# Sliding-window half of a decode attention kernel, regrouped from four units of four heads to two units of eight

## The chip, the cores and the metric

The kernel runs on one core of a Trainium2 chip. A core has a matrix engine (PE, with its weight loads listed as PEld), a vector engine (VectorE, DVE in the profile), a scalar engine (ScalarE, ACT), GpSimd (POOL) and a synchronisation engine (SyncE, SP), which here issues nearly all transfers. The engines have instruction streams of their own and wait for one another on semaphores. Sixteen DMA engines move data from device memory to the on-chip memory of 128 partitions; matmul results go to eight accumulation banks of 128 x 512 floats. The metric is the device time of one execution in microseconds (us), lower is better.

## What is computed

Two independent attention layers for one new token, A and B, of the same sizes: 576 inputs, 32 query heads, 16 key-value heads of 128 channels, a cache of 8192 keys in bf16. A looks only at the last 2048 keys, B at all.

```python
B, Sq, D = 1, 1, 576
Hq, Hkv, Sk, Dh = 32, 16, 8192, 128
W = min(4096, max(256, Sk // 4))        # A only: 2048
q = (x @ wq) as 32 heads of 128
k = jnp.repeat(k_cache[:, :, Sk - W:, :], 2, axis=1)   # B: all of k_cache
v = jnp.repeat(v_cache[:, :, Sk - W:, :], 2, axis=1)
scores = jnp.einsum("bhqd,bhkd->bhqk", q, k) * (Dh ** -0.5)
p = softmax(scores)
o = jnp.einsum("bhqk,bhkd->bhqd", p, v)
return o.reshape(B, Sq, Hq * Dh) @ wo   # A and B side by side: 1152 numbers
```

The bytes that must be read are A's and B's wq and wo, 8.4 MB each of K and V for A (16 heads x 2048 keys x 128 channels x 2 bytes), and 33.6 MB each of K and V for B.

## The kernel before

**Order of work.** The class `Prog` (L39) collects operations by engine; each engine runs its list in the order in which the program appended it, and `emit` (L61) turns named dependencies into semaphore waits. So the order of the calls at L466 to L492 is the order on every engine.

**Loads.** `place` (L172) hands out space in `ring`, 73728 bf16 columns on 128 partitions, from left to right, going back to 0 when a piece would not fit. A load waits for the last users of the space that it overwrites. All of these loads are issued by SyncE in one order: wo of A (its first part, in a buffer of its own), the two parts of wq for A and B, then K and V of the units as L234 to L237 give it (K of unit i, then V of unit i-1), then the rest of wo. Since one queue takes them all, a load that waits on SyncE holds up the ones behind it.

**Units.** A unit is a group of key-value heads, four of A or four of B (L213); units 0 to 3 are A's and 4 to 7 are B's. A partition of an A unit holds head p % 4 and 64 keys in one row of 16 KB (L222), in a single load of 2 MB for K and for V. A B unit has rows of 64 KB, K in two loads of 4 MB and V in one of 8 MB, the last unit's V in two. A load is named by kind and unit, with its half: K5.1 is the second half of K of unit 5.

**Slabs.** A unit's row is worked in slabs of 2048 columns, that is 16 keys a partition: four slabs for an A unit, sixteen for a B unit. For each slab VectorE transposes K (`turn`, L360) in 32 x 32 blocks into one of three slots of `ktb`; PE then multiplies it (`score`, L367) by four shifted views of the query in `za` or `zb`, so that each slab's scores fall on rows of their own in one bank of 128 x 512 floats. For A a first matmul (L373) with `mkl` and `mkr` puts a large negative number wherever query head and key head do not belong together.

**Softmax of a unit.** `peak` (L394): the maximum over the bank (max) on VectorE and a transposing matmul (mT) on PE. `spread` (L401): VectorE takes the maximum by query head (mr) and scales it (mx), PE spreads it to all partitions (bc). `expo` (L414): ScalarE copies it (nb) and takes the exponential into `psb`, with a running sum. `turnp` (L424): VectorE transposes p into `pta` (A) or `pts` (B). `pv` (L436): four matmuls a slab, each with 32 columns of p and 512 columns of V, into four groups of 32 rows of one bank. `take` (L450) copies the bank to `xo` on ScalarE, and `fold` (L455) adds the groups up on PE.

**How units overlap.** While a unit goes through its softmax, K of the next one is transposed and scored: in the loop at L469, one slab after `peak`, one after `spread`, one after `expo`, and the rest after `turnp`. Only then, in PE's order, come the PV matmuls of the unit, so a V buffer comes free after the scores of the next unit.

**Ends.** Before the units, q is made by matmuls as wq lands (L315 to L331), copied by ScalarE, transposed by VectorE (L332) and put into `za` (L338) and `zb` (L343); the first K transpose waits for both. After them the sums are inverted (L496 to L513) and the output is multiplied by wo (`final`, L518), part by part as wo lands.

Of the kernel before, what the change touches and what calls it, by code (L numbers as in the profile page):

```python
# [11 lines left out]
HQ = 32  # L12
# [11 lines left out]
TA = 4 * W_A // 128  # L24
# [3 lines left out]
ZA = 128 + 24  # L28
# [71 lines left out]
def bass_concat_heads__sliding_block_cached__gqa_block_cached__decode_kernel(nc, A_x, A_k_cache, A_v_cache, A_wq, A_wo,  # L100
# [21 lines left out]
    za = nc.alloc_sbuf_tensor("za", [128, NQ, 4, ZA], BF16)  # L122

    mkl = nc.alloc_sbuf_tensor("mkl", [4, 16, 4, 2], BF16)
    mkr = nc.alloc_sbuf_tensor("mkr", [4, 128, 4], BF16)
    mx = nc.alloc_sbuf_tensor("mx", [128, 8], F32)
    mr = nc.alloc_sbuf_tensor("mr", [128, 8], F32)

    pta = nc.alloc_sbuf_tensor("pta", [128, NA, 16, 8], BF16)
    rsa = nc.alloc_sbuf_tensor("rsa", [128, NQ], F32)  # L130
    clsa = nc.alloc_sbuf_tensor("clsa", [128, 8], F32)
    mexp = nc.alloc_sbuf_tensor("mexp", [1, 128], F32)
    nb = nc.alloc_sbuf_tensor("nb", [128, 4], F32)
    psb = nc.alloc_sbuf_tensor("psb", [128, 512], BF16)
# [4 lines left out]
    sel = nc.alloc_sbuf_tensor("sel", [128, 32], F32)  # L139
    par = nc.alloc_sbuf_tensor("par", [128, 2], F32)  # L140
# [72 lines left out]
    UNITS = [(side, u) for side in "AB" for u in range(NQ)]  # L213
# [3 lines left out]
    def load_kv(kind, i):  # L217
        side, u = UNITS[i]
        c = (ks if kind == "K" else vs)["AB".index(side)]
        use = "T%d.%d" if kind == "K" else "V%d.%d"  # L220
        if side == "A":
            src = bass.AP(tensor=c.tensor, offset=c.offset + (4 * u * SK + SK - W_A) * DH,  # L222
                          ap=[[TA * DH, 32], [SK * DH, 4], [1, TA * DH]])
            kv_at[kind, i] = [place(TA * DH, [use % (i, NA - 1)], lambda e, t: e.dma_start(t, src), "%s%d.0" % (kind, i))]
            return
        rows = c[0, 4 * u:4 * u + 4, :, :].rearrange("h (q t) d -> (h q) (t d)", q=32)
        n = 2 if kind == "K" or i == NU - 1 else 1
        kv_at[kind, i] = []
        for half in range(n):
            src = rows[:, half * ROW // n:(half + 1) * ROW // n]  # L230
            kv_at[kind, i].append(place(ROW // n, [use % (i, (half + 1) * NB // n - 1)],
                                        lambda e, t, src=src: e.dma_start(t, src), "%s%d.%d" % (kind, i, half)))
# [41 lines left out]
    op("pool", lambda e: e.tensor_copy(mkr[:], view(ident, 128, 0, [[0, 128], [1, 4]], 4)), deps=["ident"], name="mkr")  # L274
# [16 lines left out]
    for k0 in range(0, KW, 4):  # L291
# [10 lines left out]
    op("dve", lambda e: e.tensor_reduce(clsa[:], view(identf, 128, 0, [[1, 8], [8, 16]]), AX.X, ALU.add),  # L302
       deps=["identf"], name="clsa")
    op("dve", lambda e: e.tensor_reduce(sel[:], view(identf, 128, 0, [[1, 32], [32, 4]]), AX.X, ALU.add),
       deps=["identf"], name="sel")
    op("dve", lambda e: e.tensor_scalar(mkl[:], view(ident, 128, 0, [[0, 16], [1, 4], [0, 2]], 4), -1.0, BIG,
# [14 lines left out]
    for n in range(8):  # L321
# [5 lines left out]
        for h in range(2):  # L327
            op("act", lambda e, n=n, h=h: e.activation(qsb[:, n, 256 * h:256 * h + 256],  # L328
                                                       banks[n][:, 256 * h:256 * h + 256], ACT.Copy),
               deps=["qmm%d" % (KW0 + n)], name="qe%d" % n if h else None)  # L330
# [6 lines left out]
    for b in range(4):  # L337
        op("dve", lambda e, b=b: e.tensor_copy(  # L338
            view(za, NQ * 4 * ZA, ZA - 128 + 32 * b, [[4 * ZA, NQ], [2 * ZA, 2], [ZA, 2], [1, 8]], 32, 32 * b),
            view(ktb, KT, 0, [[1024, NQ], [64, 2], [1, 2], [128, 8]], 32, 32 * (b % 2))),  # L340
            deps=QT + ["za0"], name="z0.%d" % b)
    for b in range(4):
        op("dve", lambda e, b=b: e.tensor_copy(  # L343
            view(zb, NQ * 4 * ZW, 32 * b + W0, [[4 * ZW, NQ], [2 * ZW, 2], [ZW, 2], [1, 2]], 32, 32 * b),
            view(ktb, KT, b * 256, [[1024, NQ], [64, 2], [1, 2], [128, 2]], 32, 64 + 32 * (b % 2))),
            deps=QT + ["zb0"], name="z1.%d" % b)
# [5 lines left out]
    sbank = [(qb if side == "A" else sb)[u % 2] for side, u in UNITS]  # L352
    vbank = [vb[1] if side == "A" else vb[0] for side, _ in UNITS]

    def prev(i):

        return [i - 2] if i >= 2 and UNITS[i - 2][0] == UNITS[i][0] else []
# [9 lines left out]
    def score(i, s):  # L367
        side, u = UNITS[i]
        k, bank = k0[i] + s, sbank[i]

        def mm(e):
            if side == "A" and s == 0:
                e.matmul(bank[:, :], lhsT=mkl[:].rearrange("p a h r -> p (a h r)"),  # L373
                         rhs=mkr[:].rearrange("p q h -> p (q h)"), start=True, stop=False)
            for c in range(2):
                for v in range(2):
                    if side == "A":
                        lhsT = za[:, u, 2 * c + v, ZA - 128 - 8 * s:ZA - 8 * s]
                    else:
                        lhsT = zb[:, u, 2 * c + v, W0 - 2 * s:W0 - 2 * s + 128]  # L380
# [3 lines left out]
                                   stop=(s == nslab[i] - 1 and c == 1 and v == 1))  # L384
            return ins
        deps = ["T%d.%d" % (i, s)]
        if s == 0:
            deps += ["mkl", "mkr"] + QE
            for n in prev(i):
                deps += ["exp%d" % n, "max%d" % n]  # L390
        op("pe", mm, deps=deps, name="S%d" % k)


    def peak(i):  # L394
        was = ["mr%d" % (i - 1), "nb%d" % (i - 1)] if i else ["identf"]
        op("dve", lambda e: e.tensor_reduce(mx[:, 0:1], sbank[i][:, :], AX.X, ALU.max),  # L396
           deps=["S%d" % (k0[i] + nslab[i] - 1)] + (["mT%d" % (i - 1)] if i else []), name="max%d" % i)
        op("pe", lambda e: e.matmul(mb[0:1, 0:128], lhsT=mx[:, 0:1], rhs=identf[:, :], start=True, stop=True),  # L398
           deps=["max%d" % i] + was, name="mT%d" % i)

    def spread(i):  # L401
        A = UNITS[i][0] == "A"
        deps = ["mT%d" % i] + (["mx%d" % (i - 1), "bc%d" % (i - 1)] if i else [])
        rows = [[1, 8], [8, 16]] if A else [[32, 4], [1, 2], [2, 16]]
        out = mr[0:1, :] if A else mr[0:1, :].rearrange("p (b r) -> p b r", r=2)
        op("dve", lambda e: e.tensor_reduce(out, view(mb, 512, 0, rows, parts=1), AX.X, ALU.max), deps=deps,  # L406
           name="mr%d" % i)
        to, of = ([[8, 16], [1, 8]], [[0, 16], [1, 8]]) if A else ([[32, 4], [2, 16], [1, 2]], [[2, 4], [0, 16], [1, 2]])
        op("dve", lambda e: e.tensor_scalar(view(mexp, 128, 0, to, parts=1), view(mr, 8, 0, of, parts=1), -SCALE, None,
# [4 lines left out]
    def expo(i):  # L414
# [3 lines left out]
           deps=["bc%d" % i] + (["exp%d" % (i - 2)] if i >= 2 else []), name="nb%d" % i)  # L418
        acc = (rsa if side == "A" else rsb)[:, u:u + 1]
        op("act", lambda e: e.activation(psb[:, :], sbank[i][:, :], ACT.Exp, bias=nb[:, c:c + 1], scale=SCALE,  # L420
                                         accum_out=acc),
           deps=["nb%d" % i, "warm1"] + (["PT%d" % (i - 1)] if i else []), name="exp%d" % i)

    def turnp(i):  # L424
        side, _ = UNITS[i]
        deps = ["exp%d" % i, "pts0"] + (["V%d.%d" % (i - 1, nslab[i - 1] - 1)] if i else [])
        if side == "A":
            op("dve", lambda e: e.transpose(view(pta, NA * 128, 0, [[8, 16], [128, NA], [1, 8]]), psb[:, :]),  # L428
               deps=deps, name="PT%d" % i)
        else:  # L430
            for b in range(4):
                op("dve", lambda e, b=b: e.transpose(  # L432
                    view(pts, NB * 128, 2 * b, [[8, 16], [128, NB], [1, 2]], 32, 32 * b), psb[32 * b:32 * b + 32, :]),
                   deps=deps, name="PT%d" % i if b == 3 else None)

    def pv(i, s):  # L436
        src, landed = slab("V", i, s)

        def mm(e):
            for j in range(4):  # L440
                if UNITS[i][0] == "A":
                    lhsT = pta[:, s, 4 * j:4 * j + 4, :].rearrange("p t k -> p (t k)")
                else:
                    lhsT = view(pts, NB * 128, 128 * s + 32 * j, [[1, 32]])
                ins = e.matmul(vbank[i][32 * j:32 * j + 32, :], lhsT=lhsT, rhs=src[:, 512 * j:512 * j + 512],  # L445
                               start=(s == 0), stop=(s == nslab[i] - 1))
            return ins
        op("pe", mm, deps=[landed, "PT%d" % i] + (["xo%d" % (i - 1)] if i else []), name="V%d.%d" % (i, s))
# [6 lines left out]
    def fold(i):  # L455
        side, u = UNITS[i]
        c, at = (1, 8 * u) if side == "A" else (0, HQ + 8 * u)

        def mm(e):
            for t in range(4):  # L460
                ins = e.matmul(ob[:, at:at + 8], lhsT=xo[:, c, 128 * t:128 * t + 128], rhs=sel[:, 8 * t:8 * t + 8],  # L461
                               start=(t == 0), stop=(t == 3))
            return ins
        op("pe", mm, deps=["xo%d" % i, "sel"], name="O%d" % i)

    for s in range(nslab[0]):  # L466
        turn(0, s)
        score(0, s)
    for i in range(NU):  # L469
# [3 lines left out]
        def ahead(m):  # L473
            for s in todo[:m]:
                turn(i + 1, s)
                score(i + 1, s)
# [10 lines left out]
        turnp(i)  # L487
# [7 lines left out]
    last = NU - 1  # L495
    op("dve", lambda e: e.tensor_tensor(  # L496
        lsel[:, 0, :].rearrange("p (u m) -> p u m", m=8), rsa[:, :].unsqueeze(2).to_broadcast([128, NQ, 8]),
        view(clsa, 8, 0, [[0, NQ], [1, 8]]), ALU.mult), deps=["exp%d" % (NQ - 1), "clsa"], name="lselA")
    op("dve", lambda e: e.tensor_tensor(
        lsel[:, 1, :].rearrange("p (u m) -> p u m", m=8), rsb[:, :].unsqueeze(2).to_broadcast([128, NQ, 8]),  # L500
        view(clsb, 8, 0, [[0, NQ], [1, 8]]), ALU.mult), deps=["exp%d" % last, "clsb"], name="lsel")
# [16 lines left out]
    def final(P, c):  # L518
# [10 lines left out]
        op("pe", mm, deps=["wo%d.%d" % (P, c), "oP", "exp%d" % (NQ - 2)], name="F%d.%d" % (P, c))  # L529
# [44 lines left out]
```

## Time and profile before

| | |
|---|---|
| median of three runs | 246.12 us (246.03 to 246.19) |
| the profiled execution | 245.95 us |
| its span, first to last instruction | 244.6 us |
| mean granted PE clock | 0.847 |
| busy: PE, VectorE, ScalarE, GpSimd | 69%, 51%, 9%, 3% |
| read from device memory | 102.76 MB, 420 GB/s over the span |
| transposes of K on VectorE (L364) | 80, 92.8 us in all |
| transposes of p for A (L428), each | 712 ns |
| maximum over an A bank (L396), each | 692 ns |
| loads of A's K and V | eight, 2048 KB each |

A page of the profile shows one execution. Its digits give the busy share in tenths in 40 slices of the span. A queue's line gives packets, megabytes and the share that its packets took of sixteen engines over the span. In the chain of waits each step is followed back to what released it; a step of a transfer lasts from its issue to its landing, so it can span other transfers that went ahead of it in the queue. A line of the timeline has the start, the duration, and in brackets the idle time of the engine before it and what ended it.

### The profile page before, as it was taken

How to read it: one execution, taken by the hardware profiler on the slowest of the kernel's cores; microseconds unless marked ns; L12 is line 12 of the kernel's file. 1: busy time of each engine (PE TensorE's matmuls, PEld its weight loads, DVE VectorE, ACT ScalarE, POOL GpSimd, SP SyncE). 2: the span in 40 equal slices, each digit the busy share in tenths (PEclk: the TensorE clock that was granted, in tenths of full speed). 3: DMA queues.
4: the chain of work that ended last, by engine and by line, in shares of the span. 5: the costliest groups of instructions: out<-in, count | busy, mean ns of one | idle time of the engine just before them, and what ended most of it. 6: DMA issues, size and time to landing. Idle time of an engine off the chain costs nothing.

```text
span 244.6 us, 2224 instructions
## 1 busy us (share of the span) xinstructions
PE 168.2 (69%) x952; PEld 69.5 (28%) x952; DVE 124.7 (51%) x156; ACT 21.5 (9%) x54; POOL 8.1 (3%) x15
## 2 busy tenths in 40 slices
PE   0059692977887799669736569938197976654696
PEld 0024240322444222323112323203052322321453
DVE  0040026677688998899700679930369960130200
ACT  2200052001121100200000010000010000200000
POOL 8400000000000000000000000000000000000000
PEclk9999899579999999979968767997855995757769
DMA  7999899999999999998989999989999999999994
GB/s 279 429 486 435 367 431 429 429 429 437 434 439 434 425 437 445 429 490 386 482 375 429 429 485 396 461 370 429 426 482 418 439 423 402 431 430 426 422 412 190
DMA packets 4369, 102.90 MB, mean 421 GB/s; under 512 B 516, under 2 KB 648, under 8 KB 904
## 3 DMA queue, kind: packets, MB, share of 16 engines
q1 hardware_dynamic: 4356, 102.76, 98.1%
q8 instruction: 7, 0.11, 0.2%
q14 instruction: 2, 0.02, 0.0%
q10 hardware_dynamic: 4, 0.00, 0.0%
HBM read 102.76 MB, written 0.00 MB: 420 GB/s over the span
## 4 chain that ended last, share of the span: by engine, by line
DMA 61%; PE 21%; DVE 12%; ACT 2%; issue 2%; SPq 2%; DVEq 0%
DMA ring<-in_B_v_cache_dram 39%; DMA ring<-in_B_wo_dram 12%; DMA ring<-in_B_wq_dram 10%; DVE ktb L364 9%; PE vb L445 7%; PE qb L381 5%; PE sb L312 2%; ACT psb L420 1%; DVE pta L428 1%; PE ob L461 1%; PE vb L312 1%; PE qb L312 1%; PE sb L381 1%; SPq L201 1%; PE qb L373 1%
## 5 line engine op out<-in xcount | busy, mean ns | idle before, releaser
L364 DVE STREAM_TRANSPOSE ktb<-ring 128x1024 int32<-128x1024 int32 x80 | 92.8, 1211 | 28.2 <-DMA ring<-in_B_k_cache_dram 27.1
L381 PE MATMUL sb<-ktb,zb 128*128 128x512 bf16 x256 | 73.2, 425 | 23.2 <-DVE ktb L364 20.5
L381 PEld LDWEIGHTS sb<-ktb,zb 128*128 128x128 bf16 x256 | 22.8, 104 | 70.1 <-DVE ktb L364 45.4
L445 PE MATMUL vb<-ring,pts 128*32 128x512 bf16 x256 | 23.6, 546 | 20.6 <-DMA ring<-in_B_v_cache_dram 16.5
L381 PE MATMUL qb<-ktb,za 128*128 128x512 bf16 x64 | 19.3, 448 | 2.8 <-DVE ktb L364 2.8
L445 PEld LDWEIGHTS vb<-ring,pts 128*32 128x32 bf16 x256 | 8.5, 130 | 35.2 <-DMA ring<-in_B_v_cache_dram 18.7
L452 ACT ACTIVATE xo<-vb 128x512 f32<-128x512 f32 x8 | 4.8, 597 | 130.3 <-PE vb L445 130.3
L432 DVE STREAM_TRANSPOSE pts<-psb 32x512 bf16<-32x512 bf16 x16 | 11.3, 704 | 7.7 <-ACT psb L420 7.5
L332 DVE STREAM_TRANSPOSE ktb<-qsb 128x512 int32<-128x512 int32 x4 | 2.8, 711 | 21.8 <-ACT qsb L328 21.8
L461 PEld LDWEIGHTS ob<-sel,xo 128*128 128x128 f32 x64 | 10.0, 226 | 3.4 <-ACT xo L452 2.1
L312 PE MATMUL sb<-ring,xrep 128*128 128x512 bf16 x18 | 7.3, 546 | 5.3 <-DMA ring<-in_B_wq_dram 5.3
L525 PE MATMUL qb<-ring,oP 128*1 128x256 bf16 (+1 forms) x112 | 10.2, 326 | 0.5 <-DMA ring<-in_B_wo_dram 0.5
L461 PE MATMUL ob<-sel,xo 128*128 128x8 f32 x64 | 9.3, 273 | 1.2 <-ACT xo L452 1.2
L381 PEld LDWEIGHTS qb<-ktb,za 128*128 128x128 bf16 x64 | 6.2, 109 | 13.3 <-issue 5.7
L287 PE MATMUL sb<-onesb,xint 1*128 1x128 bf16 x8 | 1.1, 307 | 11.7 <-ACT xint L283 11.7
L525 PEld LDWEIGHTS qb<-ring,oP 128*1 128x1 bf16 x112 | 5.9, 90 | 4.8 <-DMA ring<-in_B_wo_dram 1.7
L539 DVE CAST outsb<-qb 1x256 bf16<-1x256 f32 x2 | 0.8, 420 | 12.1 <-PE qb L525 12.1
L505 DVE RECIPROCAL rl<-mb 128x64 f32<-128x64 f32 x1 | 0.6, 557 | 12.3 <-PE mb L502 12.3
L295 DVE TENSOR_SCALAR xrep<-sb,par 128x256 bf16<-128x256 f32 x4 | 1.7, 477 | 10.1 <-PE sb L287 10.1
L373 PE MATMUL qb<-mkr,mkl 4*128 4x512 bf16 x4 | 1.8, 439 | 7.2 <-DVE ktb L364 7.2
L406 DVE TENSOR_REDUCE mr<-mb 1x8 f32<-1x128 f32 x8 | 1.9, 241 | 9.4 <-PE mb L398 9.4
L396 DVE TENSOR_REDUCE mx<-qb 128x1 f32<-128x512 f32 x4 | 2.8, 692 | 6.3 <-PE qb L381 6.3
(70 smaller groups left out, 86.2 us busy)
## 6 DMA issues: line engine op xcount, KB each, us to landing
ring<-in_B_k_cache_dram SPq DMA_DIRECT2D x8, 4096.0 KB, 24.1
ring<-in_A_k_cache_dram SPq DMA_DIRECT2D x4, 2048.0 KB, 32.6
ring<-in_A_v_cache_dram SPq DMA_DIRECT2D x4, 2048.0 KB, 26.2
ring<-in_B_v_cache_dram SPq DMA_DIRECT2D x2, 4096.0 KB, 23.8
ring<-in_A_wo_dram SPq DMA_DIRECT2D x1, 3456.0 KB, 21.4
ring<-in_A_wq_dram SPq DMA_DIRECT2D x1, 2560.0 KB, 19.4
ring<-in_B_wq_dram SPq DMA_DIRECT2D x1, 2560.0 KB, 24.7
ring<-in_B_wo_dram SPq DMA_DIRECT2D x1, 2448.0 KB, 26.8
```

What stands on the lines that cost most here:

```text
L201: return e.dma_start(bass.AP(tensor=ring, offset=P * RING + lo, ap=[[2 * RING, 64], [1, (k1 - k0) * w]]), src)
L312: return e.matmul(banks[n][:, :], lhsT=xrep[:, k, :], rhs=wq_at[k][:, n * 512:(n + 1) * 512], start=(k == 0), stop=(k == KW - 1))
L332: op("dve", lambda e, n=n: e.transpose(ktb[:, (n - 1) * 512:(n + 1) * 512].bitcast(I32), qsb[:, n - 1:n + 1, :].rearrange("p a n -> p (a n ...
L364: op("dve", lambda e: e.transpose(kt.bitcast(I32), src.bitcast(I32)), deps=[landed] + (["S%d" % (k - NKT)] if k >= NKT else Z), name="T%d. ...
L373: e.matmul(bank[:, :], lhsT=mkl[:].rearrange("p a h r -> p (a h r)"), rhs=mkr[:].rearrange("p q h -> p (q h)"), start=True, stop=False)
L381: ins = e.matmul(bank[:, :], lhsT=lhsT, rhs=view(ktb, KT, (k % NKT) * SLAB + 64 * c + v, [[128, 16], [2, 32]]), start=(side == "B" and s = ...
L396: op("dve", lambda e: e.tensor_reduce(mx[:, 0:1], sbank[i][:, :], AX.X, ALU.max), deps=["S%d" % (k0[i] + nslab[i] - 1)] + (["mT%d" % (i - ...
L432: op("dve", lambda e, b=b: e.transpose(view(pts, NB * 128, 2 * b, [[8, 16], [128, NB], [1, 2]], 32, 32 * b), psb[32 * b:32 * b + 32, :]), ...
L445: ins = e.matmul(vbank[i][32 * j:32 * j + 32, :], lhsT=lhsT, rhs=src[:, 512 * j:512 * j + 512], start=(s == 0), stop=(s == nslab[i] - 1))
L452: op("act", lambda e: e.activation(xo[:, c, :], vbank[i][:, :], ACT.Copy), deps=["V%d.%d" % (i, nslab[i] - 1)] + (["O%d" % (i - 1)] if i e ...
L461: ins = e.matmul(ob[:, at:at + 8], lhsT=xo[:, c, 128 * t:128 * t + 128], rhs=sel[:, 8 * t:8 * t + 8], start=(t == 0), stop=(t == 3))
L525: ins = e.matmul(fb[r:r + 1, 0:hi - lo], lhsT=oP[:, P, k0 + k:k0 + k + 1], rhs=wo_at[P, c][:, k * DM + lo:k * DM + hi], start=(k0 + k == 0 ...
```

## The change

A's sixteen heads are worked in two units of eight heads. Partition 8g + h holds head h of the unit and 128 keys in one row of 32 KB; K and V of a unit are loads of 4 MB. A slab is still 16 keys a partition, so a unit has eight slabs. With sixteen query rows for a slab, two slabs fill a bank, and a unit's scores take four banks, shared in turn with the banks that the projection, B's scores and B's PV use elsewhere in the kernel. Each bank has a mask matmul, a maximum, an exponential and a transpose of its own; a further maximum (top) joins the four. `psb` becomes two of the slots of `qsb`, used in turn. PV of A uses two groups of 64 columns in place of four groups of 32, so a group takes two matmuls of each slab. The copies into `zb` go from four on VectorE to eight on ScalarE, and a reduction (`rta`) adds the four partial sums of each A unit before the inverse is taken. Units 0 and 1 are now A's, 2 to 5 are B's.

```diff
-TA = 4 * W_A // 128
+HA = 8
+UA = G // HA
+TA = HA * W_A // 128
 NA = TA * DH // SLAB
-ZA = 128 + 24
+RA = 2 * HA
+SB = 2
+NBK = NA // SB
+WA = RA * (SB - 1)
+ZA = 128 + WA
...
-    psb = nc.alloc_sbuf_tensor("psb", [128, 512], BF16)
+    psb = qsb
...
-    UNITS = [(side, u) for side in "AB" for u in range(NQ)]
+    UNITS = [(side, u) for side in "AB" for u in range(UA if side == "A" else NQ)]
...
-            src = bass.AP(tensor=c.tensor, offset=c.offset + (4 * u * SK + SK - W_A) * DH,
-                          ap=[[TA * DH, 32], [SK * DH, 4], [1, TA * DH]])
+            src = bass.AP(tensor=c.tensor, offset=c.offset + (HA * u * SK + SK - W_A) * DH,
+                          ap=[[TA * DH, 128 // HA], [SK * DH, HA], [1, TA * DH]])
...
     for b in range(4):
-        op("dve", lambda e, b=b: e.tensor_copy(
-            view(zb, NQ * 4 * ZW, 32 * b + W0, [[4 * ZW, NQ], [2 * ZW, 2], [ZW, 2], [1, 2]], 32, 32 * b),
-            view(ktb, KT, b * 256, [[1024, NQ], [64, 2], [1, 2], [128, 2]], 32, 64 + 32 * (b % 2))),
-            deps=QT + ["zb0"], name="z1.%d" % b)
+        for c in range(2):
+            op("act", lambda e, b=b, c=c: e.activation(
+                view(zb, NQ * 4 * ZW, 32 * b + W0 + 2 * ZW * c, [[4 * ZW, NQ], [ZW, 2], [1, 2]], 32, 32 * b),
+                view(ktb, KT, b * 256 + 64 * c, [[1024, NQ], [1, 2], [128, 2]], 32, 64 + 32 * (b % 2)), ACT.Copy),
+                deps=QT + ["zb0"], name="z1.%d" % b if c else None)
...
-    sbank = [(qb if side == "A" else sb)[u % 2] for side, u in UNITS]
+    for i, (side, u) in enumerate(UNITS):
+        sbank.append([sb[u % 2]] if side == "B" else [(sb[0], vb[0])[u % 2], qb[0], qb[1], sb[1]])
+        before.append([user.get(id(t), []) for t in sbank[i]])
+        nexp.append([sum(map(len, sbank[:i])) + j for j in range(len(sbank[i]))])
+        for j, t in enumerate(sbank[i]):
+            user[id(t)] = ["exp%d.%d" % (i, j), "max%d.%d" % (i, j)]
...
+    def high(i, j):
+        to = mx[:, j:j + 1] if len(sbank[i]) > 1 else mx[:, 4:5]
+        op("dve", lambda e: e.tensor_reduce(to, sbank[i][j][:, :], AX.X, ALU.max),
+           deps=["S%d" % (k0[i] + per(i) * (j + 1) - 1)] + (["mT%d" % (i - 1)] if i else []) +
+           (["top%d" % (i - 1)] if len(sbank[i]) > 1 and i else []), name="max%d.%d" % (i, j))
+
+    def step(i, s):
+        turn(i, s)
+        score(i, s)
+        if s >= 2 * per(i) - 1 and (s + 1) % per(i) == 0:
+            high(i, (s + 1) // per(i) - 2)
...
+        for j, bank in enumerate(sbank[i]):
+            q = nexp[i][j]
+            acc = rsa[:, u, j:j + 1] if side == "A" else rsb[:, u:u + 1]
+            op("act", lambda e, q=q, acc=acc, bank=bank: e.activation(
+                psb[:, q % 2, :], bank[:, :], ACT.Exp, bias=nb[:, c:c + 1], scale=SCALE, accum_out=acc),
+               deps=["nb%d" % i, "warm1"] + (["PT%d.%d" % psof[q - 2]] if q >= 2 else []), name="exp%d.%d" % (i, j))
...
                 if UNITS[i][0] == "A":
-                    lhsT = pta[:, s, 4 * j:4 * j + 4, :].rearrange("p t k -> p (t k)")
+                    lhsT, w, g = pta[:, s, 4 * j:4 * j + 4, :].rearrange("p t k -> p (t k)"), 8 * HA, 2
                 else:
-                    lhsT = view(pts, NB * 128, 128 * s + 32 * j, [[1, 32]])
-                ins = e.matmul(vbank[i][32 * j:32 * j + 32, :], lhsT=lhsT, rhs=src[:, 512 * j:512 * j + 512],
-                               start=(s == 0), stop=(s == nslab[i] - 1))
+                    lhsT, w, g = view(pts, NB * 128, 128 * s + 32 * j, [[1, 32]]), 32, 4
+                ins = e.matmul(vbank[i][w * (j % g):w * (j % g) + w, :], lhsT=lhsT, rhs=src[:, 512 * j:512 * j + 512],
+                               start=(s == 0 and j < g), stop=(s == nslab[i] - 1 and j >= 4 - g))
...
-        turnp(i)
+        for j in range(len(sbank[i])):
+            turnp(i, j)
+            if j % 2 and j < len(sbank[i]) - 1:
+                ahead(1)
...
+    op("dve", lambda e: e.tensor_reduce(rta[:], rsa[:], AX.X, ALU.add), deps=["exp%d.%d" % (UA - 1, NBK - 1)],
+       name="rta")
```

## The prediction

> **What bounds the kernel now.** I read the queues, the digits of the slices and the chain of waits on the page first, then the chain in order of time for its end, then SyncE's issues one by one with the times to landing, and last the timeline from 42 to 98 us, where the change lies.
>
> ```profile
> DMA  7999899999999999998989999989999999999994
> q1 hardware_dynamic: 4356, 102.76, 98.1%
> q8 instruction: 7, 0.11, 0.2%
> DMA 61%; PE 21%; DVE 12%; ACT 2%; issue 2%; SPq 2%; DVEq 0%
> 212.06 29.56 DMA ring<-in_B_wo_dram
> 241.66 1.33 PE qb L525 x12
> 243.01 0.43 ACT outsb L537
> ```
>
> The reader is to see one thing: queue q1 is busy for 98.1% of 16 engines over the span, that is 240.0 of 244.6 us, and the missing 4.6 us lie at the two ends, about 2 us before the first bytes and 3 us after the last. The DMA digits are low only in the first and last slice. The chain ends in the last weights of wo, a matmul, a copy and the store. PE, VectorE and ScalarE stand in that chain only because it hops over them while transfers run behind; their share is not time that can be won. So 102.76 MB through a full queue is the kernel's time, and an edit of the computation counts only if it (a) alters how fast those bytes pass, or (b) delays a load's issue until the queue has run dry.
>
> The margin for (b) is read from SyncE's issues and their landings (columns: start, duration; the other three are one issue each, the last number is us to landing):
>
> ```profile
> 98.02 0.33 SPq L232 DMA_DIRECT2D ring<-in_B_v_cache_dram  x1
> ring<-in_A_v_cache_dram SPq DMA_DIRECT2D x1, 2048.0 KB, 24.7
> ring<-in_B_k_cache_dram SPq DMA_DIRECT2D x1, 4096.0 KB, 20.1
> ring<-in_B_v_cache_dram SPq DMA_DIRECT2D x1, 28.4
> ```
>
> The second is V2, issued at 38.50 and landed at 63.2; the third is K5.1, issued at 86.91 and landed at 107.0; the fourth is V4, issued at 98.02 and landed at 126.4. V4 is the tightest load of the kernel: it is issued 9.0 us before the transfer ahead of it has landed. Every other load after the start has 10 us or more, by the same reckoning (K5.1 itself: issued at 86.91, the load ahead landed at 97.3).
>
> **Bytes and rows.** A's loads go from eight of 2 MB in rows of 16 KB to four of 4 MB in rows of 32 KB; the bytes stay. By the landings, V1, K3 and V2 landed at 53.4, 58.3 and 63.2, so 4.9 us each; B's K halves, 4 MB in 32 KB rows, landed at 97.3 and 107.0, so 9.7 us. Eight times 4.9 is 39.2, four times 9.7 is 38.8: a gain of at most 0.4 us as rounded. The trace's packet records give it finer: by the first of the 16 engines to finish, the eight A loads took 4.86 to 4.89 us each, 39.02 in all, and a B half 9.71, so 38.84 for four: 0.18 us. Their mean packets give the other end: 617 ns for 16 KB and 1218 ns for 32 KB, so 64 x 617 - 32 x 1218 = 0.51 us an engine. I take 0.2, since landings count the overlap of neighbouring packets and single packets do not. On the low side nothing excludes a small loss (below).
>
> **Front end.** z1 (eight ScalarE copies in place of four VectorE copies, 0.79 us in all) now runs beside z0 (1.23 us). An ACT of such a size is bounded by nb's 0.17 us (128x1) and the 0.33 us of a 128x256 copy; at 0.2 it is 8 x 0.23 = 1.85 from 39.92, so the first transpose starts at 41.8 instead of 42.10; at 0.33 it starts at 42.6. Worth nothing either way, as the queue is full until 47 with loads already issued.
>
> **A's computation, walked for when slots come free.** With the ring of 73728 columns the new order places K0 at 36864, K1 at 53248, V0 at 0 (over wq), K2.0 and K2.1 at 16384 and 32768, V1 at 49152, K3.0 at 0, K3.1 at 16384, V2 at 32768 (unit 2 is now B's first). So K2.1 waits for the transposes of K0, V1 for those of K1, K3.0 for PV of unit 0, K3.1 for the first eight transposes of K2, and V2 for the rest of them and for PV of unit 1. From there the places and waits are as before. The bytes ahead of V2 equal those ahead of V4 before, so the queue runs dry at the same moments: 65.8 for K2.1, 75.5 for V1, 85.2 for K3.0, 94.9 for K3.1, 104.8 for V2 (first engine done; the last one 106.6), from the packet records of before with the loads put in the new order.
>
> Rows for the walk:
>
> ```profile
> 58.50 1.05 PE L445 MATMUL vb<-ring,pta 128*32 128x512 bf16 x16
> 58.61 0.69 DVE L396 TENSOR_REDUCE mx<-qb 128x1 f32<-128x512 f32 x1 [1.14 <-PE qb L381]
> 60.51 0.39 PE L373 MATMUL qb<-mkr,mkl 4*128 4x512 bf16 x1 [0.75 <-DVE ktb L364]
> 63.21 0.69 ACT L420 ACTIVATE psb<-qb,nb 128x512 bf16<-128x512 f32 x1
> 64.02 0.71 DVE L428 STREAM_TRANSPOSE pta<-psb 128x512 bf16<-128x512 bf16 x1 [0.88 <-ACT psb L420]
> 81.13 14.72 DVE L364 STREAM_TRANSPOSE ktb<-ring 128x1024 int32<-128x1024 int32 x13
> ```
>
> A transpose of K costs 14.72/13 = 1.13 us of VectorE, a max 0.61 to the next start, a transpose of p 0.63, an exp 0.81 until its transpose starts, a score slab 4 x 0.215 on PE (0.43 a matmul until about 49 us, while PE is slow), a mask matmul 0.32 more. The change adds four exps, four transposes of p, four maxima, two tops and four masks, and drops two rounds of mT, mr, mx, bc, nb and two folds. Added on VectorE: 4 x 0.63 + 4 x 0.61 + 2 x 0.25 = 5.5, dropped 2 x 0.5.
>
> New waits: the scores of unit 1 in banks 1 to 3 wait for unit 0's exps of those banks. Slab (1,2) waits for the second exp, till 60.1; behind it on PE stand only later slabs, and for those VectorE's sixth K transpose of unit 1, which is not due before 64.9. The third exp waits for the first p-transpose, as psb has two buffers; behind it on ScalarE stands the fourth.
>
> PV is the operation that no row shows. A slab was four matmuls of 32 columns, and 16 took 1.05 us: at 0.215 for 512 columns that is four at a time. Four matmuls of 64 columns cost 0.215 a slab if still all four overlap, 0.86 if none does. I take 0.43, two at a time, since the nearest row shows the array shared by as many as fit side by side. [...]
>
> The legs: first transpose 41.9; eight slabs, five at slow PE and three at VectorE's pace with two maxima, scores of unit 0 done 54.5; max, top, mT, one slab, mr, mx, bc, nb, exp, first p-transpose at 59.3; four p-transposes, one K transpose and a max, 63.9; four K transposes (last done 69.0) and two maxima, scores of unit 1 done 70.2; PV of unit 0, 8 x 0.43, done 73.6; mT (queued behind PV on PE), slab, fold, bc, nb, four exps against four p-transposes and one slab, 80.8; twelve K transposes at 1.13, 94.4; the last scores and PV of unit 1 (1.0 + 3.5), 98.9. The same walk made for before ends at 96.7 where the trace has 97.95, because PE there stays slow for one slab longer; so 1.3 goes on every time past 55. Result: K2.1 issued at 53.4 (dry at 65.8), V1 at 70.3 (75.5), K3.0 at 74.9 (85.2), K3.1 at 86.7 (94.9), V2 at 100.2 (104.8). An issue reaches the engines about 1.0 us later (first issue 0.73, first packet 1.76). All are in time; what covers A's longer computation is this queue, and V2's cover shrinks from 6.8 to 4.6 us. If it were gone, each us late would be a us of the end.
>
> **The rest.** The new sum over rsa (rta, about 0.2 us on VectorE, as the neighbours of its size) runs near 216, where VectorE idles 12.3 us until the reciprocal at 228.8. The final matmuls wait on wo's bytes as before. Sum: 245.95 for the profiled execution less 0.2, and that execution lies 0.17 below the median of 246.12. I give 245.9 against the median.
>
> **Rivals.** About 0.2% (0.5 us) is what a measurement here can tell from no change. (1) Slower: PV in 64 columns does not overlap. Then both PVs take 3.4 us more each, V2 is issued at 107.1, its bytes start at 108.1, and the last engine has idled since 106.6: 1.5 us, so 247.4. It decides from a V2 issue of 105.6 on, 5.4 us later than I walk. For it: no row of 64 columns. Against: the fourfold overlap of 32. 11%. (2) PE keeps its 0.43 pace through unit 1 and PV: 8 x (1.72 - 1.13) + 2 x 3.4 = 11.5 us later, less the 5.4 of cover, about 252; half of that is likelier, 247. For it: PE clocks of 5 to 9 tenths in the page; against: it was 1.00 from 59 to 98 us. 6%. (3) Instruction fetches. Each of q8's seven packets held up one DMA engine by some 1.5 us in the packet records (the load in flight at 47.1 had its last engine 1.1 us behind the next one), on a different engine each time, and the slowest engine sets the end. PE goes from 1904 instructions to about 1864, so seven stay; should two hit one engine, 247.5. 4%. [...] (4) The eight heads of one group lie 2 MB apart, so rows that neighbouring partitions read could collide in memory. Four heads did so before, at 4.9 us per 2 MB against 4.85 for B: 1% of 39 us. If doubling the heads made that 5%, 2 us more: 248. 4%. [...] (5) Faster: the packet means hold (0.51) or the slowest engine escapes a fetch (0.3 more): 245.3. 15%. (6) The rows stay cut into 16 KB packets and nothing changes at all: 246.1, 3%; B's 32 KB rows go as one packet each, which speaks against it.
>
> **Numbers.** Forecast 57%, with 245.6 to 246.4 as its own range. Faster 15% (5); within 0.2% 60% (forecast and 6); slower 25% (1 to 4). From 245.3 to 247.5 the range holds the forecast, most of (5), and (1) and (3).
>
> **What would show it.** Right: q1 near 98% again, some 576 packets fewer (512 rows and 4 x 16 completions), no low DMA digit before the last slice, V2 issued at 99 to 102 right after PV of unit 1. Wrong: a DMA digit of 8 or less near 104 to 109 us, PV slabs of 0.86, 4 MB of A landing more than 9.8 us apart, or one engine landing 3 us after the others.

## The result: 42 us slower, and the profile after

The changed kernel takes 288.24 us (median of 6 runs, 287.89 to 289.51) against 246.05 us (245.98 to 246.19) for the kernel before: a ratio of 1.1722, 95% interval 1.1701 to 1.1744. The forecast was 245.9 us, no change.

From the page of the changed kernel, its span, DMA digits, rates, queue line and the row of A's two K loads (the digits and rates cover 40 slices of 7.2 us; the row has the size of a load and the median us to landing):

```profile
span 287.3 us, 2188 instructions
DMA  8999999999999999999999989999899999999994
GB/s 310 438 456 347 219 219 219 217 214 201 201 193 360 438 431 214 205 228 429 424 484 438 431 365 438 502 414 429 388 433 433 481 420 401 420 429 430 420 418 187
q1 hardware_dynamic: 3780, 102.76, 98.2%
ring<-in_A_k_cache_dram SPq DMA_DIRECT2D x2, 4096.0 KB, 54.5
```

The same megabytes, 576 packets fewer, and the queue as full as before, 98.2%. But in slices 5 to 12 and 16 to 18 it moves 193 to 228 GB/s, half of the 430 elsewhere. The queue did not run dry; its packets took twice as long. By the first engine to finish (the packet records), A's four loads took 19.5, 19.9, 19.9 and 19.7 us, 79.1 in all, against 39.0 for the eight loads before: 40.1 us. The two loads of B that follow one of A's took 10.8 us each instead of 9.7, 2.2 us more. That sums to 42.3 us. The medians differ by 42.2, the two profiled executions (288.62 and 245.95) by 42.7.

From the page's chain that ended last, its shares by engine, and from its costliest groups the transposes of K (busy time, mean of one, idle time before them and what ended it), with the same group of the kernel before as the last line:

```profile
DMA 76%; PE 14%; DVE 4%; another core or an unknown queue 3%; SPq 1%; ACT 0%; issue 0%
...
L384 DVE STREAM_TRANSPOSE ktb<-ring 128x1024 int32<-128x1024 int32 x80 | 92.8, 1211 | 68.6 <-DMA ring<-in_B_k_cache_dram 54.8
...
L364 DVE STREAM_TRANSPOSE ktb<-ring 128x1024 int32<-128x1024 int32 x80 | 92.8, 1211 | 28.2 <-DMA ring<-in_B_k_cache_dram 27.1
```

The transposes cost what they did, 1211 ns each, and VectorE's idle time before them has grown from 28.2 to 68.6 us, by 40.4: it waits for bytes. Two pieces of the chain in order of time (start, duration, what):

```profile
3.73 44.33 DMA ring<-in_A_k_cache_dram
...
83.75 45.73 DMA ring<-in_A_v_cache_dram
```

K0 lands only at 48.1, and V1, issued at 83.75, at 129.5. The computation now waits for A's bytes, which before it never did after the start.

A stretch well inside K0 and K1, all engines' work beside the DMA share and rate (columns: stretch, length, busy time of PE, its weight loads, VectorE, ScalarE and GpSimd, granted clock, DMA share, GB/s), and below it a stretch of the kernel before in which only A's loads pass:

```profile
45.00:55.00 10.00, 5.61 (x14) 1.63 (x15) 6.19 (x6) 0.00 (x0) 0.00 (x0) 0.52 1.00 210
...
28.00:48.00 20.00, 15.06 (x51) 5.77 (x52) 9.42 (x16) 5.26 (x16) 0.00 (x0) 0.76 1.01 432
```

The share is 1.00 in both, the rate 210 GB/s against 432. In the packet records of this time every one of the 16 engines is at work, with 16 packets in flight, and a 32 KB packet takes 2.56 us (median; 2.30 to 2.57), where B's take 1.22.

### The profile page after: what moved, and what is told of

Its sections match the earlier page's. It is cut to its first block, busy times and chain, and to the rows that moved or that the text cites. A ratio compares the mean times of both kernels' runs of the same rounds, so it can differ in the third digit from the quotient of the medians.

```text
span 287.3 us, 2188 instructions
## 1 busy us (share of the span) xinstructions
PE 182.5 (64%) x932; PEld 72.8 (25%) x932; DVE 128.7 (45%) x160; ACT 23.9 (8%) x66; POOL 7.1 (2%) x15
## 3 DMA queue, kind: packets, MB, share of 16 engines
q1 hardware_dynamic: 3780, 102.76, 98.2%
## 4 chain that ended last, share of the span: by engine, by line
DMA 76%; PE 14%; DVE 4%; another core or an unknown queue 3%; SPq 1%; ACT 0%; issue 0%
DMA ring<-in_B_v_cache_dram 35%; DMA ring<-in_A_v_cache_dram 16%; DMA ring<-in_A_k_cache_dram 15%; DMA ring<-in_B_wo_dram 10%; PE vb L485 8%; DVE ktb L384 3%; PE sb L403 2%; PE qb L403 1%; DVE pta L467 1%; SPq L209 1%; DVE mx L415 1%; PE vb L403 1%; PE qb L568 0%; SPq L253 0%
## 5 line engine op out<-in xcount | busy, mean ns | idle before, releaser
L384 DVE STREAM_TRANSPOSE ktb<-ring 128x1024 int32<-128x1024 int32 x80 | 92.8, 1211 | 68.6 <-DMA ring<-in_B_k_cache_dram 54.8
L403 PE MATMUL sb<-ktb,zb 128*128 128x512 bf16 x256 | 78.3, 445 | 29.4 <-DVE ktb L384 26.3
L485 PE MATMUL vb<-ring,pts 128*32 128x512 bf16 x256 | 25.3, 578 | 19.8 <-DMA ring<-in_B_v_cache_dram 15.8
L485 PE MATMUL vb<-ring,pta 128*64 128x512 bf16 x64 | 10.5, 499 | 10.6 <-DMA ring<-in_A_v_cache_dram 10.6
L472 DVE STREAM_TRANSPOSE pts<-qsb 32x512 bf16<-32x512 bf16 x16 | 11.3, 703 | 9.5 <-ACT qsb L458 9.3
L485 PEld LDWEIGHTS vb<-ring,pta 128*64 128x64 bf16 x64 | 4.5, 143 | 16.6 <-DMA ring<-in_A_v_cache_dram 11.6
L403 PE MATMUL qb<-ktb,za 128*128 128x512 bf16 x32 | 8.1, 390 | 0.4 <-DVE ktb L384 0.4
L415 DVE TENSOR_REDUCE mx<-sb 128x1 f32<-128x512 f32 x7 | 4.8, 692 | 6.3 <-PE sb L403 6.3
L403 PE MATMUL sb<-ktb,za 128*128 128x512 bf16 x24 | 7.4, 461 | 0.0
L467 DVE STREAM_TRANSPOSE pta<-qsb 128x512 bf16<-128x512 bf16 x8 | 5.3, 693 | 3.7 <-ACT qsb L458 3.7
L501 PEld LDWEIGHTS ob<-sel,xo 128*128 128x128 f32 x32 | 5.8, 262 | 3.1 <-ACT xo L492 2.4
L501 PE MATMUL ob<-sel,xo 128*128 128x8 f32 x32 | 5.5, 301 | 1.2 <-ACT xo L492 1.2
```

The source lines that it names most:

```text
L384: op("dve", lambda e: e.transpose(kt.bitcast(I32), src.bitcast(I32)), deps=[landed] + (["S%d" % (k - NKT)] if k >= NKT else Z), name="T%d. ...
L403: ins = e.matmul(bank[:, :], lhsT=lhsT, rhs=view(ktb, KT, (k % NKT) * SLAB + 64 * c + v, [[128, 16], [2, 32]]), start=(side == "B" and s = ...
L415: op("dve", lambda e: e.tensor_reduce(to, sbank[i][j][:, :], AX.X, ALU.max), deps=["S%d" % (k0[i] + per(i) * (j + 1) - 1)] + (["mT%d" % (i ...
L467: op("dve", lambda e: e.transpose(view(pta, NA * 16 * RA, SB * 16 * RA * j, [[RA, 16], [16 * RA, SB], [1, RA]]), psb[:, q, :]), deps=deps, ...
L472: op("dve", lambda e, b=b: e.transpose(view(pts, NB * 128, 2 * b, [[8, 16], [128, NB], [1, 2]], 32, 32 * b), psb[32 * b:32 * b + 32, q, :] ...
L485: ins = e.matmul(vbank[i][w * (j % g):w * (j % g) + w, :], lhsT=lhsT, rhs=src[:, 512 * j:512 * j + 512], start=(s == 0 and j < g), stop=(s ...
```

## The experiments

The first theory was rival 4 of the prediction made large: rows of eight heads, 2 MiB apart, collide in memory. Its rivals were the length of the rows and the new computation. A's loads alone were edited; the computation around them stayed.

**Contiguous rows (e1_contig).**

```diff
-            src = bass.AP(tensor=c.tensor, offset=c.offset + (HA * u * SK + SK - W_A) * DH,
-                          ap=[[TA * DH, 128 // HA], [SK * DH, HA], [1, TA * DH]])
+            src = bass.AP(tensor=c.tensor, offset=c.offset + HA * u * SK * DH,
+                          ap=[[HA * TA * DH, 128 // HA], [TA * DH, HA], [1, TA * DH]])
```

> The changed kernel with A's four loads reading 4 MB of neighbouring bytes (partition pitch 32 KB) in place of eight heads 2 MiB apart; sizes, rows, places, waits and computation stay, the keys read are others, so the output is not the reference's. Theory (address collision: only the distance between rows read at one time matters): the A loads take 9.7 us each instead of 19.5 to 19.9, time 246 us. Rival (row length of 32 KB, the new computation, or its buffers): 288 us stays.

Measured: 245.69 us. The same window, now at full rate:

```profile
45.00:55.00 10.00, 9.28 (x32) 2.78 (x29) 8.42 (x9) 0.00 (x0) 0.00 (x0) 0.81 1.03 441
```

So rows of 32 KB, the new computation, its banks and waits cost nothing; the whole loss is in how A's bytes are loaded.

**A skew of one chunk (e2_skew32k).** The head pitch becomes `SK * DH + TA * DH`.

> The changed kernel with the head pitch of A's loads at 2 MiB + 32 KB, so that neighbouring partitions read neighbouring chunks of different heads; eight heads are still read at once. The keys read are others than the window's. Theory (collision of equal offsets modulo a power of two): 246 us. Rival (eight regions far apart are slow whatever their offsets): 288 us.

Measured: 289.17 us. Unequal offsets don't help, against the theory as far as offsets modulo a power of two go.

**The kernel before with eight heads (e3_before_8h).**

```diff
...
-                          ap=[[TA * DH, 32], [SK * DH, 4], [1, TA * DH]])
...
+                          ap=[[TA * DH, 16], [SK * DH, 8], [1, TA * DH]])
```

> The kernel before, with A's eight loads of 2 MB in 16 KB rows reading eight heads x 16 chunks in place of four heads x 32 chunks; it computes on the wrong heads. Theory (eight rows at equal offsets collide, row length is innocent): each A load takes 9.8 us instead of 4.9, time 246 + 39 = 285 us. Rival (32 KB rows are what is slow): 246 us.

Measured: 286.21 us, 217 GB/s between 30 and 45 us. The row length is innocent from the other side as well: 16 KB rows halve too. The number agrees with the theory, but the shape 16 x 8 changed along with the eight heads.

**Heads outside, chunks inside (e4_outer_heads).** `ap=[[SK * DH, 16], [TA * DH, 8], [1, TA * DH]]`.

> The changed kernel with partition 8a + b of an A load reading head a (16 heads) and chunk b (8 chunks of 32 KB); it computes on the wrong heads. It tells how partitions are dealt to the 16 DMA engines. Dealt in turn (partition modulo 16): at one time two heads x eight chunks are read, no more than two rows at equal offsets, 246 us. Eight neighbouring partitions to an engine: sixteen heads at equal offsets at one time, at least as slow as the change, 288 to 365 us.

Measured: 288.89 us, as slow as the change, though heads and chunks have changed places. Every slow kernel so far had a source of 16 x 8 rows. The contiguous one, written with the same two counts, is one run of 128 equal steps. That made a second theory: the shape decides, through the partitions that each DMA engine writes; by it the next run stays at 288 us.

**A source of 16 x 8 with nothing far apart (e5_near_contig).** `ap=[[(HA + 1) * TA * DH, 128 // HA], [TA * DH, HA], [1, TA * DH]]`, which differs from e1 by a gap of one row after every eight.

> The contiguous variant with a gap of 32 KB after every eight rows, so that the source keeps its two levels of 16 x 8 rows but lies within 4.7 MB; the keys read are others. Source theory (rows 2 MiB apart collide in memory): 246 us, as nothing is far apart. [...]

Measured: 288.82 us.

```profile
45.00:55.00 10.00, 5.69 (x17) 1.85 (x18) 6.35 (x6) 0.00 (x0) 0.00 (x0) 0.59 1.01 210
```

The reader is to see 210 GB/s at a DMA share of 1.01, as in the change. The first theory falls here: nothing is 2 MiB apart, and the rate is halved all the same.

**The shapes 32 x 4 and 64 x 2 (e6_32x4, e7_64x2).** `ap=[[TA * DH, 32], [SK * DH, 4], [1, TA * DH]]` and `ap=[[TA * DH, 64], [SK * DH, 2], [1, TA * DH]]`, rows of 32 KB.

> The changed kernel with A's loads shaped 32 x 4: four heads 2 MiB apart, 32 chunks of 32 KB each, the shape of before with the rows of the change; it computes on other keys and heads. Shape theory (engines share out 32 outer indices of four partitions as they share out 128 rows): 9.7 us a load, 246 us. Source theory (far rows of 32 KB collide): slower, towards 288 us.

> A's loads shaped 64 x 2: two heads 2 MiB apart, 64 chunks of 32 KB; it computes on other keys and heads. Theory (an engine's partitions are given by the shape only where an outer index has more than four partitions): 246 us. [...]

Measured: 245.72 and 245.66 us, with these windows:

```profile
45.00:55.00 10.00, 9.00 (x33) 2.77 (x31) 8.82 (x11) 0.00 (x0) 0.00 (x0) 0.86 1.04 444
45.00:55.00 10.00, 9.19 (x32) 2.80 (x30) 8.47 (x10) 0.00 (x0) 0.00 (x0) 0.82 1.04 447
```

Heads are 2 MiB apart and rows 32 KB long as in the change, and the rate is full. So the shape 16 x 8 halves the rate, and neither the distance in memory nor the length of a row does.

**Which partitions are written (e8_halves, e9_even_odd).** Each A load of e1 becomes two of 64 rows. The halves (partitions 0 to 63, then 64 to 127) have `step, p1 = 1, 64`, even and odd `2, 1`. The step and the start count for the rows of memory as well as for the partitions. If such loads pass at half the rate, A's 39 us are spent twice, 246 + 39 = 285 us.

```diff
+            def half(e, t, h):
...
+                src = bass.AP(tensor=c.tensor, offset=off + h * p1 * TA * DH, ap=[[step * TA * DH, 64], [1, TA * DH]])
+                return e.dma_start(bass.AP(tensor=ring, offset=h * p1 * RING + lo, ap=[[step * RING, 64], [1, TA * DH]]), src)
...
+            step, p1 = 1, 64
```

> The contiguous variant with each A load issued as two of 64 rows, partitions 0 to 63 and then 64 to 127; same bytes, same rows of memory. [...] Source theory: nothing changes, 246 us.

> The same with the two loads taking the even and then the odd partitions, 64 rows each. [...] If 64-row loads are slow whatever their partitions: 285 us, as with the halves.

Measured: 289.29 us for the halves, 245.69 us for even and odd. Their windows, first the halves:

```profile
45.00:55.00 10.00, 5.42 (x12) 1.47 (x13) 6.00 (x6) 0.00 (x0) 0.00 (x0) 0.50 1.01 210
```

and then even and odd:

```profile
45.00:55.00 10.00, 9.18 (x32) 2.79 (x30) 8.48 (x10) 0.00 (x0) 0.00 (x0) 0.83 1.04 447
```

Both read the same 4 MB for each load in rows of the same length; what differs is which 64 rows, and so which 64 partitions, go together. The slow loads have no distance in memory in common: it was 2 MiB between heads in the change, 32 KB between neighbouring rows in e8. The partitions that are written together are what is left, and that is an argument; no run kept the source of a load and changed the partitions alone.

For the 16 x 8 load this suggests an account that no run shows in its parts. Suppose that engine e gets outer index e, so partitions 8e to 8e + 7, and walks them in order. Then all engines stand at the same place of their eight at every moment, and the 16 partitions that are written together lie eight apart. The account is that rows written in this step halve each other; why they should was not shown. It needs the engines to be in step, which the next three runs tested.

**A lead for half of the engines (e10_lead, e13_lead_dram, e14_lead_dram_half).** All three are the change as it is, plus two transfers ahead of K0 whose data is not used; in e10 and e13 they are to put groups of engines 4.9 us apart, four rows of 32 KB.

```diff
...
+    for n, k in enumerate((4, 12)):
+        load("sp", lambda e, k=k, n=n: e.dma_start(
+            bass.AP(tensor=idle.tensor, offset=idle.offset + n * 96 * 8192, ap=[[8 * 8192, k], [8192, 8], [1, 8192]]),
+            bass.AP(tensor=ks[1].tensor, offset=ks[1].offset, ap=[[9 * 8192, k], [8192, 8], [1, 8192]])),
+            s_lead, 32, name="lead%d" % n)
```

This is e13; e10 wrote into K1's space instead, and e14 has rows of 4096 columns.

> The changed kernel as it is, with two idle transfers put ahead of A's first load, whose data is not used: one shaped 4 x 8 rows of 16 KB and one of 12 x 8. If an outer index goes to one engine, lowest engines first, engines 0 to 3 get 16 more rows of 16 KB (9.8 us), 4 to 11 get 8 (4.9 us) and 12 to 15 none. [...] Theory (in step is what halves the rate): A's loads pass at full rate, 9.7 us each, and the end is that of the engines with the most bytes: 246 + 9.8 = 256 us. Rival (a 16 x 8 load is slow for another reason, such as a limit of each engine): 288 + 5 to 10 = 293 to 298 us.

> [...] Here they go from device memory to device memory and nothing waits for them; again 4 x 8 and 12 x 8 rows of 16 KB, not used. [...] If the lead comes to eight rows, a whole load, the engines are in step again, 298 us. Rival (a limit that has nothing to do with the step): K0 to V0 19.5 us each, 293 to 298 us.

> The same with idle rows of 8 KB, half the lead. If a copy within device memory passes at half the rate of a load, this one is the four-row lead (256 to 265 us) and the one before is the whole load; if it passes at the full rate, this lead is two rows, half of the time in step: about 270 to 280 us. Rival: 290 to 293 us.

Measured: 298.74, 284.72 and 293.79 us. The totals don't bear the theory out: e10 and e14 lie just above the rival's ranges, and e13 lies between the 256 to 265 us given for a lead of four rows and the rival's range. They also carry the idle rows, in e13 twice 4.9 us on four engines. The stages say more. Three windows of e13, in the first two of which K0, K1 and the start of V0 pass, shaped 16 x 8 as in the change:

```profile
37.00:47.00 10.00, 1.01 (x5) 0.28 (x3) 2.16 (x6) 2.60 (x12) 0.00 (x0) 0.69 1.00 423
47.00:57.00 10.00, 8.08 (x23) 2.49 (x24) 8.55 (x9) 0.00 (x0) 0.00 (x0) 0.63 1.05 418
57.00:67.00 10.00, 7.37 (x32) 2.52 (x30) 9.22 (x13) 2.73 (x8) 0.00 (x0) 1.00 0.99 210
```

The very loads that pass at 210 GB/s in the change pass at 423 and 418 here. In the packet records the idle rows put twelve completions at 31.7 to 32.1 us and the last four near 36.6, so the counts 4 and 12 did set the number of engines. The page agrees: e13 has 16 packets under 512 B more than the changed kernel (468 against 452), one completion for each outer step. K0 then completes in three groups: on four engines at 36.9 to 37.1, on eight at 41.4 to 41.8, on four at 46.4 to 46.8, when the four ahead complete K1. So the groups are about four rows of 1.22 us apart, as intended. So a 16 x 8 load is not slow through a limit of each engine alone: how the engines stand to each other decides.

Two findings speak against the simple form of the account, in which only engines at the same place halve each other. In e14, with a lead of two rows, A's loads pass at 208 to 214 GB/s from 37 to 87 us; its first two windows:

```profile
37.00:47.00 10.00, 1.42 (x7) 0.45 (x5) 2.56 (x6) 2.63 (x12) 0.00 (x0) 0.76 0.98 210
47.00:57.00 10.00, 3.56 (x9) 1.09 (x9) 4.61 (x4) 0.00 (x0) 0.00 (x0) 0.50 0.98 210
```

The author's estimate was that half the lead leaves the engines in step half of the time, so that half of the rows pass at full rate; but from 30 to 84 us no 32 KB packet of e14 took less than 2.07 us. And in e13 the rate falls back to 210 at 57 us, when the engines ahead enter K2.0, a load of another shape. Eight engines finish V0 from 65.4 us on and the other four not before 74.4, so these two groups were still about four rows apart; yet between 57.5 and 66 us every 32 KB packet took 2.29 us or longer. In e10 K1's issue was over only at 45.1 us and some engines stood idle before it (DMA share 0.85 from 37 to 42 us), which may have cost part of the lead; the rate was 342, 262 and 293 GB/s in the three stretches of 10 us from 42 to 72, then 212 and 226 in the page's slices from 74 to 89. That the shape of the load sets the rate is shown; what exactly makes the engines halve each other stays open.

**The rest of the change, timed (e11_contig_timed).** e1 again, executed more often.

> The contiguous variant again, timed against the kernel before, for the size of what the prediction took for the whole of the change (rows of 32 KB, half as many loads, the new computation). The prediction's term: 0.2 us faster, by its packet means 0.5. First look of this variant and of the 32 x 4 shape: 0.3 to 0.4 us.

Measured: 245.77 us (11 runs) against 246.07 (15 runs), a ratio of 0.9989, interval 0.9980 to 0.9998: 0.3 us faster, between the two sizes that the prediction had for this term.

This size belongs to e1, which reads other keys. None of the kernels run here has eight heads a unit, the right keys and the full rate. With eight heads in one level of a load and the 16 chunks of the window in the other, a load of 128 rows has 16 or 8 on the outside. The shape 32 x 4 is that of the kernel before, with its rows of 16 KB.

## Why the prediction was wrong, step by step

- **What bounds the kernel: half right.** Bytes through q1 are the time, before and after. But "a full queue" was read as "as fast as bytes can pass". The busy share counts packets in flight however long they take: 98.2% at 358 GB/s mean. The share needed the rate and the duration of a packet beside it. Two of the prediction's signs of being right, q1 near 98% and 576 packets fewer, came with 42 us more, so they could not tell.
- **Bytes and rows: this step failed.** It priced A's new loads at 9.7 us, from B's K halves, because size and row length were the same: "eight times 4.9 is 39.2, four times 9.7 is 38.8". B's half is one level of 128 rows, A's new load two levels of 16 x 8, the load of before 32 x 4. The shape stood in the diff, `ap=[[TA * DH, 128 // HA], [SK * DH, HA], [1, TA * DH]]`, and no row of the trace had it. For PV, which no row showed either, the prediction worked out a time for each overlap; the shape of the load got no such bounds, only the words that a small loss is not excluded, and rival 4. It measured 19.8 us a load, 79.1 for the four in place of 38.8. The prediction's own sign of being wrong, 4 MB of A landing more than 9.8 us apart, came: K0, K1 and V0 landed some 20 us apart. All 16 engines do work on these loads, at half speed: 16 packets in flight, each 2.56 us in place of 1.22.
- **Rival 4 named the right transfers, with the wrong cause and price.** It blamed the distance in memory (e5 refutes that: 288.82 us with rows close together; e6 and e7 too: full rate at 2 MiB) and set 2 us where the loads lost 40. That four heads passed at 4.9 us per 2 MB was used as evidence about heads; it was evidence about the shape 32 x 4.
- **The walk for when slots come free: right.** With the loads at full rate (e11), SyncE issued K2.1, V1, K3.0, K3.1 and V2 at these times:

```profile
52.14 0.33 SPq L240 DMA_DIRECT2D ring<-in_B_k_cache_dram  x1
68.44 0.33 SPq L232 DMA_DIRECT2D ring<-in_A_v_cache_dram  x1
73.19 0.33 SPq L240 DMA_DIRECT2D ring<-in_B_k_cache_dram  x1
84.81 0.33 SPq L240 DMA_DIRECT2D ring<-in_B_k_cache_dram  x1
98.58 0.33 SPq L240 DMA_DIRECT2D ring<-in_B_v_cache_dram  x1
```

  The walk had 53.4, 70.3, 74.9, 86.7 and 100.2. All are early by 1.3 to 1.9 us; the last four, without the correction of 1.3 that was added past 55 us, are within 0.6. No load came late: V2 is issued 6 us before the 104.8 at which the walk had the queue run dry, and the DMA share is 1.00 from 97 to 107 us.
- **PV in 64 columns: right.** From the timeline of e11, the last 24 matmuls of PV of unit 1:

```profile
95.72 2.76 PE L485 MATMUL vb<-ring,pta 128*64 128x512 bf16 x24
```

  That is 0.115 us each with the drain at the end, 0.46 a slab, so two at a time where one alone takes 0.215 (in the trace of before a slab's score matmuls of 128 columns start 0.215 to 0.221 us apart once the clock is full); rival 1 is out. Rival 2 is out for e11 too: PE's granted clock was 0.95 and 0.88 in the stretches of 10 us from 47 and 57 us, and 1.00 from 67 to 107. In the changed kernel itself, where PE waits for V, the 32 matmuls of a unit's PV take 5.05 and 5.40 us, the second at a granted clock of 0.66.
- **Front end: right.** From the same timeline:

```profile
39.72 1.39 ACT L356 ACTIVATE zb<-ktb 32x16 bf16<-32x16 bf16 x8 [0.78 <-DVE ktb L344]
39.72 1.25 DVE L350 COPY za<-ktb 32x128 bf16<-32x128 bf16 x4
41.24 2.37 DVE L384 STREAM_TRANSPOSE ktb<-ring 128x1024 int32<-128x1024 int32 x2 [0.27 <-ACT zb L356]
```

  The copies run side by side and the first K transpose starts at 41.24 instead of 42.10 (41.8 was forecast), worth nothing, as said.
- **The sum without its failed step** was 0.2 us faster with 0.5 as the other end, and measured 0.3 in e11 (interval 0.05 to 0.5 us).

## What to carry to other kernels

When a load's access pattern changes, compare its levels, not only its bytes and row length: here a source of 16 x 8 rows ran at half the rate of 32 x 4, 64 x 2 or a single level of 128. Two loads of 64 rows ran at full rate on even and odd partitions and at half on the two halves. And a queue at 98% says that transfers are in flight, not that they are fast: read its GB/s by slice and the time of a packet of known size.

## What the runs showed of the hardware

- Loads of 4 MB into the same 128 partitions pass at 210 or at 441 to 447 GB/s from 45 to 55 us by the shape of the source (e5 against e1, e6 and e7), or by which 64 rows and partitions go together (e8 against e9).
- A lead of four rows (4.9 us) from one group of engines to the next, in groups of 4, 8 and 4, let the slow loads pass at 418 to 423 GB/s for 20 us (e13); a lead of two rows left them at 208 to 214 (e14).
- The number of outer steps set the number of engines: idle transfers of 4 and 12 outer steps put completions on four and twelve engines (e13).
- A copy within device memory passed at the rate of B's loads: in e13, the 128 KB of eight neighbouring 16 KB rows went as two packets of 64 KB and took 4.8 us, 27 GB/s an engine, on twelve engines at once; a 64 KB packet of B's loads took 2.42 us in the changed kernel, the same 27.
